# Decayed linear attention and a highway layer on one Trainium2 core: query layout, decay factors, store shapes and a new order of all engines

## The chip, the cores and the metric

The kernel runs on one core of a Trainium2 chip. The metric is the device time of one execution in microseconds. The engines of the core work side by side, each through its own queue in order: TensorE (PE; its weight loads are shown as PEld), VectorE (DVE), ScalarE (ACT), GpSimd (POOL) and SyncE (SP), which here only issues DMAs. Sixteen DMA engines move the data.

## The reference

Four batches, eight heads, 768 positions, 64 features a head, all in float32. `lam` holds one decay factor for each head.

```python
for b in range(nb):                       # strips of 64 positions
    intra = einsum('bhic,bhjc->bhij', qb, kb) * Dmask      # lam ** (i - j) for i >= j, else 0
    intra = einsum('bhij,bhjd->bhid', intra, vb)
    inter = einsum('bhid,bhde->bhie', qb * lam_pow, kv_state)
    out[:, :, sl] = intra + inter
    kv_state = lam_block * kv_state + einsum('bhsd,bhse->bhde', kb * rev_pow, vb)
...
x = out.transpose(0, 2, 1, 3).reshape(3072, 512)
H = maximum(x @ w_h, 0);  T = sigmoid(x @ w_t + b_t)
return T * H + (1 - T) * x
```

The decay between two positions is split in the kernels: queries are scaled by lam to the power of their position in the batch, values by its inverse, so that masks need only ones and zeros and the state needs no decay of its own.

## The kernel before, in words

The 3072 rows are worked on as twelve tiles n of 256 rows; three tiles make a batch. A tile has two halves b of 128 rows, and an operation on "p" 0 or 1 is on half of the heads, on 2 on all of them. What runs on which engine, and in which order, is written out by hand in the string `PLAN`: a loop at the end of the kernel reads its tokens one by one and calls the function that `DO` names, so each engine's queue holds its operations in the plan's order. `@` names the engine, `=` the PSUM banks (seven of them, 0 to 6). Buffers in SBUF are taken in turn, `BUFS` many of a kind; an operation that reuses one waits until the earlier use is over.

For one tile:

- `Lk`, `Lq`, `Lv` (line 173) load keys, queries and values, in two transfers of 256 KB each, as rows of 512 B (two positions of one head). All go through SP's queue, as do the weights (`W`, line 177) and the stores (`ST`, lines 337 and 356).
- `CK` casts the keys to bf16 (line 103 on DVE and POOL, 101 on ACT, which all copies share), `CQ` and `CV` scale queries and values by the decay factors (line 190).
- `TK`, `TQ` transpose keys and queries on TensorE (line 204) and `EK`, `EQ` copy the result from PSUM to `kT` and `qT`.
- `SS` is sixteen score matmuls (line 216) with sixteen matmuls of the running state `kv` between them (line 221), `KE` copies the state out to `ss`. For tile 0 scores and states stand apart as `S` and `U`. `M` masks the scores on DVE (line 255).
- `I` (line 271) and `A` (line 281) make the attention's output, transposed, in PSUM; `D` copies it to `xT`.
- `F.n.u.w` is a block of the highway layer for half of the features, eight matmuls (line 300; w is 0 for `w_h` and 1 for `w_t`). `H` makes max(h, 0) - x (line 305), `G` the sigmoid (line 314), `X` their product `th` (line 318). The last tile's halves are two groups, 11 and 12.
- `R` turns x + th back to rows by matmuls with the identity (line 347; 327 for the last tile), `E` copies them to `o`, `ST` stores them.

`WC` casts the weights, once. `Z.r` is r matmuls of a blank tile, which nothing reads (`spin`, line 366). `B` and `BC` make a column of the bias, `PT` loads the table for the sigmoid. Before the plan starts, lines 106 to 135 make the identity, the mask `tri` and the tables `pow_q` and `pow_v`: `lam` is loaded into all 128 partitions (line 107), its logarithm is multiplied with the positions (line 130), and two Exp follow (lines 133 and 135).

The PSUM tile of an attention output has its 128 columns in the order (parity of the position, pair), because a partition holds two neighbouring positions; `take` puts them in order:

```python
copy(eng, new(("xT", *g), ...)[:, :, r * C:(r + 1) * C].rearrange("p n (q j) -> p n j q", j=J),
     get("o", n, b).rearrange("p n (j q) -> p n j q", j=J))
```

Of the kernel before, what the change touches and what calls it, by code (L numbers as in the profile page):

```python
# [418 lines left out]
```

## Time and profile before

| | |
|---|---|
| median of 3 runs | 109.11 us (108.66 to 109.51) |
| profiled execution: span from its first to its last instruction | 109.3 us; the page gives no other time of it, and the span stands 0.2 us above the runs' median |
| granted TensorE clock, mean | 1.000 |
| HBM read and written | 20.98 MB and 6.29 MB, 249 GB/s over the span |
| `kf`, `vf`, `qf`: one load of 256 KB, issue to landing | 5.5, 5.4, 5.5 us |
| `w_f`: one load of 512 KB | 6.6 and 8.5 us |
| `out_dram<-o`: one store of 512 KB | 4.7 us |
| `m` on DVE, 48 times | 682 ns each |
| `qb` and `vs` on POOL, 128x1024 | 1904 ns each |
| `kT` and `qT` on ACT, 128x1024 | 1036 and 1023 ns |
| `xT` on ACT, 128x512 | 749 ns |

How to read the profile: an engine's digit is its busy share in one fortieth of the span. Matmuls are pipelined, so a busy TensorE may still have room. The chain of waits is followed back from the last instruction to what released each step. A group's line gives engine, operation, what it writes and reads, how often, busy time and mean, and the idle time before it with its releaser. A timeline line gives start, length, and the idle time before it in brackets.

### The profile page before, as it was taken

To read this page: it belongs to the slowest core of one execution; us is meant where nothing else is said; L and a number is where in the kernel's file an instruction comes from. 1 tells how busy PE (TensorE), PEld (TensorE's weight loads), DVE (VectorE), ACT (ScalarE), POOL (GpSimd) and SP (SyncE) were. 2 spreads that over 40 slices of the span, in tenths; PEclk is the share of its full clock that TensorE was granted. 3 is DMA by queue.
4 is the path that set the end of the run, shared out by engine and by line. 5 is a ranking of instruction groups with operands and counts; after the bars stand their busy time and mean duration, and the time that the engine had idled before them with its cause. 6 is when DMAs were issued, how large, how long until landed. Compare 5 with 4: busy or idle time off the path is not lost.

```text
span 109.3 us, 4968 instructions
## 1 busy us (share of the span) xinstructions
PE 99.4 (91%) x2188; PEld 80.6 (74%) x2190; DVE 82.7 (76%) x140; ACT 71.9 (66%) x129; POOL 55.7 (51%) x46
## 2 busy tenths in 40 slices
PE   4986989899999999999999999998999599999950
PEld 1343654688887878889899889896888478899940
DVE  1241595878998696999977989999858958958960
ACT  3304263787866489499579749975696758776940
POOL 6029420427979858959468296499691600000000
PEclk9999999999999999999999999999999999999999
DMA  0899999999999999989999999599999413207264
GB/s 5 233 304 290 291 366 386 312 290 287 290 266 304 287 250 262 302 228 289 296 300 293 305 341 270 181 346 326 321 333 323 170 69 125 73 6 296 94 233 151
DMA packets 42701, 27.59 MB, mean 252 GB/s; under 512 B 1588, under 2 KB 38712, under 8 KB 42680
## 3 DMA queue, kind: packets, MB, share of 16 engines
q1 hardware_dynamic: 42528, 27.27, 85.1%
q8 instruction: 17, 0.28, 1.2%
q14 instruction: 4, 0.03, 0.1%
q10 hardware_dynamic: 152, 0.01, 0.1%
HBM read 20.98 MB, written 6.29 MB: 249 GB/s over the span
## 4 chain that ended last, share of the span: by engine, by line
PE 61%; DMA 11%; DVE 6%; POOL 5%; ACT 5%; issue 4%; SPq 4%; POOLq 0%; DVEq 0%
PE bt L300 15%; PE bh L300 13%; DMA qf<-in_q_dram 11%; PE bs L216 7%; PE bo L281 5%; PE bx L347 5%; PE bspin L366 4%; PE bqtr L204 4%; DVE m L255 3%; SPq L173 3%; PE bktr L204 3%; POOL qb L190 3%; PE bo L271 3%; ACT qT L101 2%; POOL vs L190 2%
## 5 line engine op out<-in xcount | busy, mean ns | idle before, releaser
L300 PEld LDWEIGHTS <-w_b 128*128 128x128 bf16 x416 | 36.3, 98 | 6.4 <-issue 1.8
L255 DVE TENSOR_TENSOR m<-bs,tri 128x512 bf16<-128x512 f32 x48 | 31.1, 682 | 3.8 <-PE bs L216 3.4
L190 POOL TENSOR_TENSOR qb<-qf,pow_q 128x1024 bf16<-128x1024 f32 (+1 forms) x13 | 23.6, 1813 | 11.2 <-DMA qf<-in_q_dram 10.6
L314 ACT ACTIVATE bt<-bt,bt_col 128x256 f32<-128x256 f32 (+1 forms) x52 | 22.0, 432 | 6.9 <-PE bt L300 4.2
L300 PE MATMUL bt<-xT,w_b 128*128 128x256 bf16 (+1 forms) x208 | 24.5, 265 | 1.3 <-ACT qT L101 1.3
L300 PE MATMUL bh<-xT,w_b 128*128 128x256 bf16 (+1 forms) x208 | 25.0, 265 | 0.2 <-issue 0.2
L190 POOL TENSOR_TENSOR vs<-vf,pow_v 128x1024 bf16<-128x1024 f32 x10 | 19.0, 1904 | 5.0 <-DMA vf<-in_v_dram 4.6
L305 DVE SCALAR_TENSOR_TENSOR hm<-bh,xT 128x512 bf16<-128x512 f32 (+1 forms) x26 | 16.5, 643 | 4.0 <-PE bh L300 2.5
L318 DVE TENSOR_TENSOR th<-bt,hm 128x512 bf16<-128x512 f32 (+1 forms) x26 | 16.5, 643 | 2.1 <-ACT bt L314 2.0
L216 PE MATMUL bs<-qT,kT 64*64 64x128 bf16 x384 | 14.2, 218 | 0.6 <-issue 0.3
L101 ACT ACTIVATE xT<-bo 128x512 bf16<-128x512 f32 x16 | 11.5, 749 | 4.6 <-PE bo L281 4.6
L103 POOL CAST kb<-kf 128x1024 bf16<-128x1024 f32 (+1 forms) x10 | 10.0, 995 | 8.1 <-DMA kf<-in_k_dram 6.8
L101 ACT ACTIVATE ss<-kv 128x512 bf16<-128x512 f32 x15 | 8.9, 595 | 7.3 <-PE bs L216 6.1
L366 PE MATMUL bspin<-blank,id 128*128 128x512 bf16 x43 | 11.8, 416 | 1.6 <-POOL id masks.py:199 1.4
L216 PEld LDWEIGHTS <-kT 64*64 64x64 bf16 x384 | 11.0, 106 | 2.9 <-issue 1.4
L101 ACT ACTIVATE o<-bx 128x512 f32<-128x512 f32 x19 | 10.4, 596 | 1.4 <-PE bx L347 1.3
L101 ACT ACTIVATE qT<-bqtr 128x1024 bf16<-128x1024 bf16 (+1 forms) x10 | 9.8, 980 | 1.8 <-PE bqtr L204 1.8
L281 PE MATMUL bo<-m,vs 64*64 64x128 bf16 x384 | 9.4, 219 | 0.7 <-DVE m L255 0.4
L221 PE MATMUL kv<-vs,kb 64*64 64x64 bf16 x320 | 9.2, 196 | 0.2 <-POOL vs L190 0.2
L366 PEld LDWEIGHTS <-id 128*128 128x128 bf16 x45 | 4.3, 105 | 6.4 <-issue 1.7
L204 PE MATMUL bqtr<-id,qb 128*128 128x128 bf16 x96 | 7.5, 220 | 0.9 <-POOL qb L190 0.9
L281 PEld LDWEIGHTS <-vs 64*64 64x64 bf16 x384 | 6.6, 106 | 2.4 <-issue 1.5
(50 smaller groups left out, 109.1 us busy)
## 6 DMA issues: line engine op xcount, KB each, us to landing
kf<-in_k_dram SPq DMA_DIRECT2D x24, 256.0 KB, 5.5
vf<-in_v_dram SPq DMA_DIRECT2D x24, 256.0 KB, 5.4
qf<-in_q_dram SPq DMA_DIRECT2D x24, 256.0 KB, 5.5
out_dram<-o SPq DMA_DIRECT2D x11, 512.0 KB, 4.7
w_f<-in_moe_w_h_dram SPq DMA_DIRECT2D x2, 512.0 KB, 6.6
w_f<-in_moe_w_t_dram SPq DMA_DIRECT2D x2, 512.0 KB, 8.5
out_dram<-oh SPq DMA_DIRECT2D x2, 128.0 KB, 2.0
out_dram<-oq SPq DMA_DIRECT2D x1, 256.0 KB
```

What stands on the lines that cost most here:

```text
L101: A.activation(dst, src, AF.Copy)
L103: ENG[eng].tensor_copy(dst, src)
L190: ENG[eng].tensor_tensor(dst, in0=get(src, n)[:, heads(p)].rearrange("p h (j d) -> p h j d", j=J), in1=pw[:, n % NST, heads(p), :, None].t ...
L204: T.transpose(t[:, i, j, :], get(x + "b", n)[:, j, h:h + 2, :], id128)
L216: T.matmul(get("s", n, e, hp // 2)[half(b), hp % 2, j, :], lhsT=get("kT", n)[half(e), hp, j, half(b)], rhs=get("qT", n)[half(e), hp, :, ha ...
L255: V.tensor_tensor(new(("m", n, e, u), [128, 2, J, C]), in0=get("s", n, e, u), in1=tri[:, None].to_broadcast([128, 2, J, C]), op=ALU.mult)
L281: T.matmul(get("o", n, b)[half(e), hp, :], lhsT=get("vs", n)[half(b), 2 * hp + e, j, :], rhs=get("m", n, e, u)[half(b), hp % 2, j, :], sta ...
L300: T.matmul(t[:, r, :], lhsT=w_b[w][:, kc, (2 * u + r) * 128:(2 * u + r + 1) * 128], rhs=get("xT", *g)[:, kc, :], start=(kc == 0), stop=(kc ...
L305: V.scalar_tensor_tensor(new(("hm", g, u), [128, 2, z * C], tag=f"hm{z}"), in0=get("h", g, u), scalar=0.0, in1=get("xT", *g)[:, 2 * u:2 * ...
L314: A.activation(dst[:, r, :], src[:, r, :], AF.Sigmoid, bias=bt_col[:, 2 * u + r:2 * u + r + 1])
L318: ENG[eng].tensor_tensor(new(("th", g), [128, NP, z * C], tag=f"th{z}")[:, 2 * u:2 * u + 2, :], in0=get("tt", g, u), in1=get("hm", g, u), ...
L366: T.matmul(t, lhsT=id128, rhs=blank, start=True, stop=True)
```

## The change

- **Queries.** A partition now holds eight consecutive positions of one head, 2 KB in a row of `qf`; the four heads of one parity lie on neighbouring partitions. One load is 128 such rows instead of 512 rows of 512 B. `cast_q`, the transposes (`turned`) and `evac_q` follow: `qT` comes out in plain order of positions, so scores, masks (`tri`), `inter` and `take` work on plain columns.
- **Decay factors.** `lam` is loaded as a 4x2 tile. Two small float32 matmuls spread it over the partitions, once by head and once by the partition's number modulo 4; one Ln works on both. Queries get a table of their own, `pow_q8`.
- **Stores.** `ST.n@S` issues a tile's store as two DMAs, of 119 and 9 partitions; tiles 0, 1, 6, 7 and 8 have it.
- **Order.** `PLAN` is new from end to end: the order of the loads and stores on SP, which engine does which copy, the banks, and the place of every operation. There are 40 `spin` matmuls instead of 45, 34 of them ahead of the first transpose, where 12 were.

The new functions `load_wc`, `cast_wc`, `trans_rows`, `evac_k_rows`, `evac_q_rows` and `scores_state_intra` are not called by this plan; with this `GROUPS` the highway layer's groups are those of before. The core of the diff:

```diff
 PLAN = """
-Lk.0.0 Lv.0.1 Lv.0.0 Lq.0.0 Lk.0.1 Lq.0.1 Lv.1.1 CK.0.0@POOL Lq.1.0 Z.12=0 TK.0.0=0 Lq.1.1 CV.0.0@DVE Lk.1.0
-CQ.0.0@POOL EK.0.0@DVE Lv.1.0 CV.0.1@DVE CK.0.1@ACT Lk.1.1 Z.11=1 TQ.0.0=1 B=2 EQ.0.0@ACT CQ.0.1@POOL W.0.1 W.0.0
-Z.6=0 TQ.0.1=3 TK.0.1=4 EQ.0.1@DVE U.0.0 EK.0.1@ACT W.1.1 S.0.0=56 KE.0.0@DVE S.0.1=01 CQ.1.2@POOL W.1.0 M.0.0.1 Z.1=3
-U.0.1 I.0=34 M.0.1.1 KE.0.1@ACT Lk.2.1 M.0.0.0 A.0.1 M.0.1.0 TQ.1.2=0 Lq.2.1 CV.1.2@DVE CK.1.2@ACT EQ.1.2@ACT Lq.2.0
-Z.8=1 TK.1.2=1 A.0.0 EK.1.2@DVE Lk.2.0 D.0.0@DVE Z.3=5 SS.1.1=56 WC.0.0.1@ACT WC.0.0.0@POOL M.1.1.0 KE.1.0@ACT
-...
+Z.2=0 B=1 Z.2=2 Lk.0.1 Z.2=3 Lk.0.0 CK.0.0@ACT Lq.0.1 CQ.0.1@POOL CK.0.1@DVE Lq.0.0 CQ.0.0@DVE Z.3=4 Lv.0.1 Lv.0.0
+Lq.1.0 CV.0.1@POOL Lq.1.1 Lk.1.1 Lk.1.0 Z.2=5 Lv.1.0 Lv.1.1 Lq.2.0 Lq.2.1 BC@DVE Z.2=6 Z.5=0 Z.16=2 Lk.2.1 TK.0.0=3
+CQ.1.2@POOL TK.0.1=4 Lk.2.0 W.0.0 W.0.1 Z.6=5 TQ.0.2=6 Lv.2.0 EQ.0.1@ACT Lv.2.1 W.1.1 CV.0.0@DVE U.0.0 EQ.0.0@ACT
+CV.1.2@POOL EK.0.1@DVE S.0.1=02 W.1.0 Lq.3.1 EK.0.0@DVE CQ.2.2@POOL WC.0.1.1@POOL KE.0.0@DVE CV.2.2@POOL S.0.0=15
+U.0.1 KE.0.1@ACT WC.1.1.0@POOL Lq.3.0 Lk.3.1 M.0.0.1@DVE M.0.1.1@DVE WC.1.1.1@POOL Lk.3.0 Lv.3.0 WC.1.0.0@POOL I.0=46
+A.0.1 TQ.1.2=3 CK.1.2@ACT TK.1.2=0 EQ.1.2@ACT M.0.0.0@DVE M.0.1.0@DVE A.0.0 Lv.3.1 EK.1.2@ACT Lk.4.0 SS.1.1=21
+M.1.1.1@DVE D.0.1@ACT Lq.4.0 D.0.0@DVE KE.1.0@ACT CK.2.2@ACT SS.1.0=53 KE.1.1@ACT I.1=06 TK.2.2=1 WC.0.0.1@ACT
+M.1.1.0@DVE CQ.3.2@POOL M.1.0.0@DVE A.1.0 M.1.0.1@DVE WC.0.1.0@DVE A.1.1 D.1.0@DVE TQ.2.2=4 WC.0.0.0@ACT F.0.1.0=2
+H.0.1@DVE EK.2.2@DVE D.1.1@ACT F.1.0.0=5 EQ.2.2@ACT Lq.4.1 F.1.1.0=3 H.1.0@DVE SS.2.0=60 M.2.0.0@DVE SS.2.1=42
+M.2.1.0@DVE KE.2.0@ACT H.1.1@DVE F.0.0.0=1 I.2=56 M.2.1.1@DVE WC.1.0.1@ACT F.1.1.1=4 F.0.1.1=3 PT@ACT G.1.1@ACT
+F.1.0.1=2 A.2.0 G.0.1@ACT G.1.0@ACT M.2.0.1@DVE A.2.1 X.1.1@DVE X.0.1@DVE CK.3.2@POOL TQ.3.2=0 X.1.0@DVE F.0.0.1=4
+D.2.1@ACT G.0.0@ACT TK.3.2=3 EQ.3.2@ACT D.2.0@DVE F.2.1.0=6 R.1=25 E.1.1@ACT H.0.0@DVE CV.3.2@POOL X.0.0@DVE R.0=14
+...
+M.8.0.1@DVE H.6.1@DVE I.8=30 CQ.9.2@POOL TQ.9.2=4 F.7.1.0=2 Lv.9.0 CV.9.2@POOL ST.1@S F.7.0.0=5 H.7.1@DVE H.7.0@DVE
+...
+X.8.0@DVE M.11.1.0@DVE ST.5 F.8.1.1=0 F.9.1.1=2 M.11.0.1@DVE F.9.1.0=5 I.11=34 G.8.1@ACT X.8.1@DVE F.10.1.1=6
+F.10.1.0=0 ST.6@S H.9.1@DVE G.9.1@ACT G.9.0@ACT X.9.0@DVE A.11.0 X.9.1@DVE A.11.1 H.10.1@DVE D.11.0@ACT R.8=51 R.9=20
+F.10.0.0=3 E.8.0@DVE F.10.0.1=5 E.8.1@ACT D.11.1@ACT F.12.0.1=1 E.9.1@DVE H.10.0@DVE G.10.1@ACT X.10.1@DVE G.10.0@ACT
+G.12.0@ACT X.10.0@DVE F.12.0.0=4 H.12.0@DVE F.11.1.1=0 X.12.0@DVE F.11.0.1=3 F.11.0.0=6 ST.8@S H.11.0@DVE R.10=54
+E.9.0@ACT ST.9 G.11.0@ACT X.11.0@DVE R.11.1.0=2 G.11.1@ACT E.11.1.0@DVE F.11.1.0=1 E.10.1@ACT F.12.1.1=6 E.10.0@ACT
+ST.11.1.0 H.11.1@DVE X.11.1@DVE ST.10 F.12.1.0=3 R.11.0.2=2 G.12.1@ACT E.11.0.2@ACT H.12.1@DVE X.12.1@DVE R.11.1.1=4
+ST.11.0.2 E.11.1.1@ACT ST.11.1.1
 """
...
-    lam_bc = singles.tile([128, H], F32)
-    A.dma_start(out=lam_bc, in_=lam.partition_broadcast(128))
+    lam_r = singles.tile([NP, 2], F32)
+    A.dma_start(out=lam_r, in_=lam.rearrange("(h e) -> h e", e=2))
...
-    tri = singles.tile([128, J, J, C // J], F32)
+    tq_i = singles.tile([128, NST, Q], I32)
+    P.iota(tq_i, pattern=[[2 * C, NST], [1, Q]], base=0, channel_multiplier=0)
+    row_i = singles.tile([128, 1], I32)
+    P.iota(row_i, pattern=[[0, 1]], base=0, channel_multiplier=1)
+    tri = singles.tile([128, J, C], F32)
     P.memset(tri, 1.0)
     for b in range(2):
         P.affine_select(out=tri[half(b)], in_=tri[half(b)], compare_op=ALU.is_ge, fill=0.0, base=0,
-                        pattern=[[-1, J], [1, J], [J, C // J]], channel_multiplier=-J)
-    tri = tri.rearrange("p j i q -> p j (i q)")
+                        pattern=[[-1, J], [1, C]], channel_multiplier=-J)
...
+    V.tensor_scalar(row_i, in0=row_i, scalar1=128 - NP, scalar2=None, op0=ALU.bitwise_and)
+    row_f = singles.tile([128, 1], F32)
+    V.tensor_scalar(row_f, in0=row_i, scalar1=float(Q // NP), scalar2=None, op0=ALU.mult)
+    tq_f = singles.tile([128, NST, Q], F32)
+    V.tensor_scalar(tq_f, in0=tq_i, scalar1=row_f, scalar2=None, op0=ALU.add)
...
+    ones = singles.tile([NP, 128], F32)
+    V.memset(ones, 1.0)
+    pick = singles.tile([NP, 128 // NP, NP], F32)
+    V.tensor_copy(pick, id_f[:, None, :].to_broadcast([NP, 128 // NP, NP]))
+    lam_d = singles.tile([NP, NP, 2], F32)
+    V.tensor_tensor(lam_d, in0=id_f[:, :, None].to_broadcast([NP, NP, 2]), in1=lam_r[:, None, :].to_broadcast([NP, NP, 2]), op=ALU.mult)
+    lam_ps = ps.tile([128, H + 2], F32, tag="b6", name="lam_ps", bufs=1)
+    T.matmul(lam_ps[:, 0:H], lhsT=ones, rhs=lam_d.rearrange("k h e -> k (h e)"), start=True, stop=True, skip_group_check=True)
+    T.matmul(lam_ps[:, H:H + 2], lhsT=pick.rearrange("k p h -> k (p h)"), rhs=lam_r, start=False, stop=True, skip_group_check=True)
+    ln = singles.tile([128, H + 2], F32)
+    A.activation(ln, lam_ps, AF.Ln)
+    p_lq = singles.tile([128, NST, 2, Q], F32)
+    V.tensor_tensor(p_lq, in0=ln[:, None, H:H + 2, None].to_broadcast([128, NST, 2, Q]),
+                    in1=tq_f[:, :, None, :].to_broadcast([128, NST, 2, Q]), op=ALU.mult)
+    pow_q8 = singles.tile([128, NST, 2, Q], F32)
+    A.activation(pow_q8, p_lq, AF.Exp)
     p_ln = singles.tile([128, NST, H, J], F32)
-    V.tensor_tensor(p_ln, in0=ln_bc[:, None, :, None].to_broadcast([128, NST, H, J]),
+    V.tensor_tensor(p_ln, in0=ln[:, None, 0:H, None].to_broadcast([128, NST, H, J]),
                     in1=tk_f[:, :, None, :].to_broadcast([128, NST, H, J]), op=ALU.mult)
-    pow_q = singles.tile([128, NST, H, J], F32)
-    A.activation(pow_q, p_ln, AF.Exp)
...
+        if x == "q":
+            nc.sync.dma_start(out=new(("qf", n), [128, 2, Q * D], F32)[:, p],
+                              in_=q[b].rearrange("(h e) (c p j) d -> c e p h (j d)", e=2, p=C // NP, j=Q)[c, p])
+            return
...
-    def scale(n, p, eng, src, dst, pw):
+    def cast_q(n, p, eng):
+        es = slice(0, 2) if p == 2 else slice(p, p + 1)
+        z = es.stop - es.start
+        ENG[eng].tensor_tensor(new(("qb", n), [128, Q, 2, D])[:, :, es].rearrange("p j e d -> p e j d"),
+                               in0=get("qf", n)[:, es].rearrange("p e (j d) -> p e j d", j=Q),
+                               in1=pow_q8[:, n % NST, es, :, None].to_broadcast([128, z, Q, D]), op=ALU.mult)
+
+    def cast_v(n, p, eng):
         z = H if p == 2 else 4
-        ENG[eng].tensor_tensor(dst, in0=get(src, n)[:, heads(p)].rearrange("p h (j d) -> p h j d", j=J),
-                               in1=pw[:, n % NST, heads(p), :, None].to_broadcast([128, z, J, D]), op=ALU.mult)
-
-    def cast_q(n, p, eng):
-        scale(n, p, eng, "qf", new(("qb", n), [128, J, H, D])[:, :, heads(p)].rearrange("p j h d -> p h j d"), pow_q)
-
-    def cast_v(n, p, eng):
-        scale(n, p, eng, "vf", new(("vs", n), [128, H, J, D])[:, heads(p)], pow_v)
+        ENG[eng].tensor_tensor(new(("vs", n), [128, H, J, D])[:, heads(p)], in0=get("vf", n)[:, heads(p)].rearrange("p h (j d) -> p h j d", j=J),
+                               in1=pow_v[:, n % NST, heads(p), :, None].to_broadcast([128, z, J, D]), op=ALU.mult)
+
+    def turned(x, n, i):
+        if x == "k":
+            return get("kb", n)[:, i % J, 2 * (i // J):2 * (i // J) + 2, :]
+        return get("qb", n)[:, i]
 
     def trans(x, n, p, bk):
-        hs = heads(p)
-        t = bank((x + "tr", n, p), bk[0], [128, (hs.stop - hs.start) // 2, J, C], BF16)
-        for i, h in enumerate(range(hs.start, hs.stop, 2)):
-            for j in range(J):
-                T.transpose(t[:, i, j, :], get(x + "b", n)[:, j, h:h + 2, :], id128)
+        cs = range(8) if p == 2 else range(4 * p, 4 * p + 4)
+        t = bank((x + "tr", n, p), bk[0], [128, len(cs), C], BF16)
+        for i, c in enumerate(cs):
+            T.transpose(t[:, i], turned(x, n, c), id128)
...
     def evac_q(n, p, eng):
-        hs = heads(p)
-        copy(eng, new(("qT", n), [128, NP, J, C])[:, hs.start // 2:hs.stop // 2], get("qtr", n, p))
+        hs = slice(0, NP) if p == 2 else slice(2 * p, 2 * p + 2)
+        copy(eng, new(("qT", n), [128, NP, 2 * C])[:, hs].rearrange("e h (p j) -> e h p j", j=Q),
+             get("qtr", n, 2).rearrange("e j (p h) -> e h p j", h=NP)[:, hs])
...
     def score(n, e, hp, j, b):
         T.matmul(get("s", n, e, hp // 2)[half(b), hp % 2, j, :], lhsT=get("kT", n)[half(e), hp, j, half(b)],
-                 rhs=get("qT", n)[half(e), hp, :, half(b)], start=True, stop=True)
+                 rhs=get("qT", n)[half(e), hp, b * C:(b + 1) * C], start=True, stop=True)
...
-                             rhs=get("qT", n)[:, hp, :, half(b)],
+                             rhs=get("qT", n)[:, hp, b * C:(b + 1) * C],
...
     def take(n, b, eng):
-        g, r = groups(n, b)
-        z = 2 if len(g) == 1 else 1
-        copy(eng, new(("xT", *g), [128, NP, z * C], tag=f"xT{z}")[:, :, r * C:(r + 1) * C].rearrange("p n (q j) -> p n j q", j=J),
-             get("o", n, b).rearrange("p n (j q) -> p n j q", j=J))
+        g, z, r = groups(n, b)
+        copy(eng, new(("xT", g), [128, NP, z * C], tag=f"xT{z}")[:, :, r * C:(r + 1) * C], get("o", n, b))
...
-    def store_r(n):
+    def store_r(n, parts):
         i = 2 * n * C
-        nc.sync.dma_start(out=out[i:i + 2 * C].rearrange("(b p) f -> p b f", p=C), in_=get("o_sb", n).rearrange("p b j f -> p b (j f)"))
+        for p in parts:
+            nc.sync.dma_start(out=out[i:i + 2 * C].rearrange("(b p) f -> p b f", p=C)[p], in_=get("o_sb", n).rearrange("p b j f -> p b (j f)")[p])
...
+        "ST": lambda a, e, bk: store_r(*a, (slice(0, 119), slice(119, C)) if e else (slice(0, C),)) if len(a) == 1 else store(*a), "B": lambda a, e, bk: bias(bk), "Z": lambda a, e, bk: spin(*a, bk),
```

## The prediction

> **What bounds the kernel now.** I read the page's busy lines first, then the chain of waits, the windows, and the timelines of the first 20 us.
>
> ```profile
> PE 99.4 (91%) x2188; PEld 80.6 (74%) x2190; DVE 82.7 (76%) x140; ACT 71.9 (66%) x129; POOL 55.7 (51%) x46
> ...
> PE   4986989899999999999999999998999599999950
> ...
> DMA  0899999999999999989999999599999413207264
> ```
>
> TensorE is busy in almost every slice, but it is not doing the kernel's work in all of them: the first slices hold the matmuls of `spin` (L366, 43 in the records), which compute nothing. DMA is full until about 85 us.
>
> ```profile
> 9.68 0.40 PE bqtr L204 x4
> ...
> 22.09 1.75 PE bh L300 x16
> ...
> 63.33 6.45 DMA qf<-in_q_dram
> ...
> 69.93 1.44 POOL qb L190
> ...
> 72.82 1.87 POOL vs L190
> ```
>
> The columns of the chain are start, length, what. It runs through TensorE, except where it leaves it at 57 to 75 us: there a query load lands late, POOL scales late, and TensorE gets its operands late.
>
> ```profile
> core 0: us, PE busy (x) PEld busy (x) DVE busy (x) ACT busy (x) POOL busy (x), PEclk, DMA share, GB/s
> 15.00:20.00 5.00, 4.61 (x77) 2.73 (x77) 3.55 (x6) 2.66 (x4) 1.04 (x2) 1.00 1.06 379
> 25.00:30.00 5.00, 5.00 (x63) 4.42 (x62) 4.22 (x6) 3.99 (x9) 4.10 (x3) 1.00 1.09 288
> 40.00:65.00 25.00, 25.00 (x632) 22.11 (x631) 22.59 (x37) 19.42 (x34) 17.70 (x12) 1.00 1.03 289
> 70.00:75.00 5.00, 4.83 (x106) 4.22 (x94) 4.99 (x9) 3.92 (x6) 4.90 (x4) 1.00 1.07 339
> 75.00:80.00 5.00, 4.78 (x151) 4.18 (x139) 3.80 (x7) 3.12 (x8) 4.05 (x3) 1.00 1.05 334
> 80.00:85.00 5.00, 4.81 (x130) 4.05 (x128) 3.88 (x7) 3.81 (x6) 2.54 (x3) 1.00 0.94 313
> 85.00:90.00 5.00, 3.74 (x92) 3.05 (x90) 3.71 (x7) 3.20 (x6) 1.78 (x1) 1.00 0.33 120
> ```
>
> From 40 to 65 us TensorE has no pause at all; between 70 and 90 it pauses for 20 - 18.16 = 1.84 us. So the time is set by three things: when TensorE starts on real work without gaps, its fixed amount of work, and the pauses. The change leaves the matmuls as they are, so only the first and the last can move.
>
> **Queries in 2 KB rows.** Loads of 512 B rows alone ran at 288 GB/s (25 to 30 us); the stretch that is mostly weights, in 2 KB rows, at 379 (15 to 20 us). The queries are 24 x 256 KB = 6.29 MB: 21.8 us of full DMA before, 16.6 after, so 5.2 us less, 0.43 us a tile; the loads of tile 8 should land some 4 us earlier. Bounds: nothing, if the 379 came from the weights' own layout, to 5.2. Of this only what ends a TensorE pause counts. In 70 to 90 us POOL waited 2.4 us for queries and 2.4 us for values (chain: 69.93, 72.82), and TensorE behind it. The pauses there are 1.84 us by busy time; a pause also hides the drain of the last matmul (eight transposes take 0.61 us alone, 0.45 in the chain, so 0.16 each), and with some four pauses that makes 2.4 us. I take all of it off: -2.4, bounds 0 to -2.4.
>
> The Trainium skill (DMA: Bandwidth & Descriptors, Specifications) gives 512 B as the smallest transfer for line rate, which speaks against any gain. The trace does not agree: 288 against 379 GB/s. By that rule the term would be 0 and the sum 2.4 us higher.
>
> **Layouts that follow.** `take` becomes a plain copy: on ACT 749 ns before, the same shape unpermuted (`ss<-kv`) 595, so -0.15 each; on DVE 730 against 682. `evac_q` now reads PSUM with a stride and writes straight. No row shows a strided PSUM read; bounds 0 to the ratio that permuting cost `take`, 749/595 = 1.26, that is +0.26 us on a 1.02 us copy; I take the upper end, since it is the same engine and type. By counts and row durations DVE gets 3.0 us less in all (two more `kT`, four more `o`; one permuted `kb` of 1.63, two `ss`, three `qT` down to one, 1.9 us of `vs` moved to POOL), ACT between -1.0 and +2.2, POOL +1.6. DVE has 26 us and ACT 37 us of slack over the span, so this is worth nothing by itself, except near the DVE pauses of 30 to 40 us (PE busy 4.82 and 4.73 of 5): -0.7, bounds 0 to -0.9.
>
> **Decay factors.** A 4x2 load, two tiny matmuls, Ln, two products, two Exp take the place of a 128-row broadcast. The old load was issued at 0.80 and waited for until 4.42. The new one has 4 pieces; the shortest landing on the page (2.0 us, `oh`) gives 2.8, the old row 4.4. I take 2.9. Four steps of 0.2 us follow, so factors are there near 4.2, before the first query (8.05 before). Hidden by that load; without the cover it would cost the 1.3 us that ACT waited for `lam`. Eight more set-up instructions on DVE and POOL (0.1 to 0.25 us each, by `tk_f`) lie under the same wait. But the two matmuls stand first on TensorE, so the spins, which began at 1.43, now wait for `lam`: 2.9 + 0.2 (product) + 0.2 (matmuls) = 3.3 us.
>
> **The start of real work.** The plan puts 34 spins before the first transpose.
>
> ```profile
> 1.43 4.05 PE L366 MATMUL bspin<-blank,id 128*128 128x512 bf16 x12 [1.43 <-POOL id masks.py:199]
> ...
> 3.54 0.15 PEld L366 LDWEIGHTS <-id 128*128 128x128 bf16 x1 [0.28 <-issue]
> 3.96 1.02 PEld L366 LDWEIGHTS <-id 128*128 128x128 bf16 x5 [0.28 <-issue]
> ```
>
> Spins came 0.43 us apart until 4 us and 0.22 after, so the clock opened 2.6 us after the first. With the same delay: 6 slow ones to 5.9, then 28 x 0.217 = 6.1: real work starts at 12.0. From there I walked the queues with the row durations. Transposes, 6 spins (1.3) and query transposes end at 14.2; two `EQ` on ACT (0.76 each) 15.9; scores, and four masks on DVE (0.62 apart) to 18.2; ACT meanwhile has KE.0.1 to 17.3, CK.1.2 to 18.3, EQ.1.2 to 19.55, EK.1.2 to 20.5, all in one queue, so SS.1.1 stands until 20.5, and behind it everything on TensorE. KE.1.0 ends at 21.9, SS.1.0 at 22.4, DVE has masks and `D` to 23.85, then a mask and a weight cast to 24.85; TQ.2.2 ends and F.0.1.0 starts at 25.25. What this needs of loads (queries and keys of three tiles, values of two, `w_h`) is 5.2 MB, 18 us at 288 GB/s from 2.4 on, so DMA does not set it.
>
> TensorE has then done 6.8 us of real work (transposes of three tiles 6 x 0.45, scores and states 2.26, inter 0.67, intra 1.14). Before had done 5.3 at 22.09 (two tiles' transposes, one intra less), and with one and three quarters of its blocks of 0.87 us the same 6.8 at 23.6. The new order is behind by 25.25 - 23.6 = **+1.7 us**. From 25 us on I see no gap in either order until 34 us.
>
> **End.** From the last FFN matmul (104.1) to the end took 5 us, with one copy of 0.25 us on DVE inside the chain; that copy is now on ACT: -0.3, bounds 0 to -0.3.
>
> **Stores of 119 and 9.** Five stores become ten issues, 0.34 us more on SP each, while SP waits for evictions anyway (L356 waited 11.5 us for DVE): 0 in the sum; see the rival.
>
> **Sum.** Against the profiled execution's span: 109.3 + 1.7 - 2.4 - 0.7 - 0.3 = 107.6. The runs' median is 109.11, 0.2 below that span, so 107.4.
>
> **Rivals.** (1) *The pauses all go.* A tile's pitches in the chain are transposes 0.90, scores with states 1.14, inter 0.45, intra 0.57, four blocks 3.48, turns 0.57: 7.1 us. Twelve, less 1.7 for what the strips at a batch's ends lack and 0.6 for the last turns, make 83. With 6.8 done at 25.25 the other 76.2 end at 101.5, and with 4.7 behind it the span is 106.2, the time 106.0; with the clock open a microsecond earlier 105.0. Between them 105.4. For: 25 us without a pause at 40 to 65. Against: at the new loads' speed DVE and ACT queues still wait in order.
>
> (2) *The pauses stay.* If those at 70 to 90 come from the order of the queues and not from loads, 109.3 + 1.7 - 0.7 - 0.3 = 110.0, and half of them 108.8. For: the longest, 1.3 us, ended with `qT` on ACT. Against: POOL's 4.8 us of waiting for DMA just before.
>
> (3) *The clock opens late.* Each further slow spin costs 0.21 us; 8 more (T = 13.7) eat the gain: 109.1. For: the spins start 1.9 us later and the trace shows one opening only. Against: it took just 2.6 us.
> The Trainium skill (TensorE: Matmul & The Clock Gate, Part 1) says that the window of about 3.4 us runs freely, so the opening can take one to nearly two windows: 8 to 16 slow spins instead of 6, a sum of 107.8 to 109.5. The trace's 2.6 us is under that.
>
> (4) *Slower: a split store runs on few DMA engines.* No row shows a DMA of 119 partitions. If its partitions are shared out evenly, 119 = 7 x 17 lets 7 of 16 engines take 17 partitions each, 34 rows of 2 KB plus 2, where 128 partitions give each engine 16. At 379 GB/s a row takes 0.0865 us on an engine: 3.1 us instead of 1.4, +1.7 a store. Two places can put it on the path: ST.1 and ST.0, ahead of the last loads, and ST.8, ahead of the last stores. From two of five it decides: 107.4 + 3.5 = 110.9; with one it is even.
> The Trainium skill (DMA: Bandwidth & Descriptors, on why a DMA increments its semaphore by 16) has this rule: the largest number up to 16 that divides the partitions, so 7 and 9; no run here shows it yet.
>
> **Chances.** Forecast 0.40; (1) 0.15; (2) 0.15; (3) 0.10; (4) 0.20. Faster by over 1% (about what a measurement of this kernel tells from no change): the forecast, less a tenth that lands within 1%, and (1): 0.52. Within 1%: that rest, (3), and the milder halves of (2) and (4): 0.23. Slower: 0.25. Range 104.6 to 111.3: from a little under (1) to a little over (4). The forecast's own range is 106.2 to 108.6.
>
> **What would show it.** Right: `qf` landing well under 5.5 us; spins to about 12 us; first `bh` near 25; PE busy 5.00 in every window from 40 to 90; POOL waiting little for DMA. Wrong: first `bh` under 23 or over 27; pauses at 70 to 90 that no load ended; long landings of `out_dram`, or loads late behind ST.1.

## The result, and the profile after

The changed kernel is slower: 114.97 us, median of 4 runs (114.12 to 116.12), against 109.31 (108.66 to 110.01). The ratio is 1.049, with a 95% interval of 1.040 to 1.059. The forecast was 107.4. (Ratios here compare undisturbed executions only; medians are of all.)

An execution's time lies 1.7 to 2.2 us above its span in all runs of this case: the profiled execution of the changed kernel has a span of 112.6 us and a time of 114.3. So the profiled execution of before, with its span of 109.3, took about 111, some 2 us more than usual. The spans of 25 unprofiled runs of before are 106.5 to 109.6, mostly near 107.2.

The page of the changed kernel, busy shares and slices:

```profile
PE 99.7 (89%) x2189; PEld 81.4 (72%) x2189; DVE 82.6 (73%) x144; ACT 71.1 (63%) x131; POOL 57.1 (51%) x49
...
PE   0999989389999939999999999799999999999940
...
DMA  2999999999999999999998889676910016544693
```

TensorE starts later and is full from about 25 us on, but for two slices, at 40 and at 71 us, where it shows a 3 and a 7. DMA is no longer full after some 60 us. The windows show the same in figures (columns as for before):

```profile
core 0: us, PE busy (x) PEld busy (x) DVE busy (x) ACT busy (x) POOL busy (x), PEclk, DMA share, GB/s
...
40.00:45.00 5.00, 3.22 (x67) 2.79 (x66) 2.98 (x6) 2.43 (x5) 4.22 (x4) 1.00 1.14 318
40.00:65.00 25.00, 23.15 (x531) 20.03 (x530) 20.25 (x33) 17.22 (x31) 17.85 (x13) 1.00 1.04 299
70.00:75.00 5.00, 4.29 (x113) 3.82 (x110) 3.83 (x6) 3.68 (x8) 4.21 (x3) 1.00 0.70 220
75.00:80.00 5.00, 5.00 (x161) 4.45 (x160) 4.54 (x9) 3.32 (x6) 2.43 (x2) 1.00 0.77 223
80.00:85.00 5.00, 5.00 (x74) 4.36 (x68) 4.54 (x8) 4.03 (x9) 2.90 (x2) 1.00 0.35 129
85.00:90.00 5.00, 4.88 (x187) 4.33 (x188) 4.93 (x9) 3.96 (x7) 0.00 (x0) 1.00 0.03 7
```

Two of the forecasts can be read off. The loads do finish earlier: DMA is 0.70 busy at 70 to 75 us, where it was 1.07, and 0.35 at 80 to 85 instead of 0.94. And from 75 to 85 us TensorE has no pause any more. But there are new ones, 1.78 us at 40 to 45 and 0.71 at 70 to 75. The chain of waits says what the first was:

```profile
39.83 0.21 PE bs L283 x7
40.04 1.78 issue
41.82 0.19 PE kv L288
```

"issue" is time in which the engine waited for nothing that the profile shows. TensorE stopped after a score matmul of tile 3, the last but one, and went on, 1.78 us later, with a state matmul of the same `SS`, whose operands had been used by the matmuls before it.

The head, in the timeline of TensorE:

```profile
3.06 0.59 PE L148 MATMUL lam_ps<-lam_d,ones 4*128 4x8 f32 x2 [3.06 <-DVE lam_d L146]
...
4.00 1.03 PE L454 MATMUL bspin<-blank,id 128*128 128x512 bf16 x2
...
5.16 8.18 PE L454 MATMUL bspin<-blank,id 128*128 128x512 bf16 x32
13.17 0.61 PE L255 MATMUL bktr<-id,kb 128*128 128x128 bf16 x8
...
21.07 0.24 PE L283 MATMUL bs<-qT,kT 64*64 64x128 bf16 x1 [1.09 <-ACT kT L107]
...
22.43 0.19 PE L288 MATMUL kv<-vs,kb 64*64 64x64 bf16 x1 [0.73 <-ACT ss L107]
...
25.70 1.47 PE L387 MATMUL bh<-xT,w_b 128*128 128x256 bf16 x12
```

The spins run from 4.0 to 13 us, the first transpose comes at 13.17 (5.99 before), two waits for ACT follow at 21 and 22 us, and the first `bh` starts at 25.70.

### Where the 3.3 us between the two profiles are

I set both traces side by side at equal amounts of TensorE's real work (transposes and everything after them). The changed kernel is behind by 2.2 us at 26 to 34 us, by 1.8 at 38.7, by 3.3 at 42.8 (the pause above), by 4.0 at 60, by 5.0 at 73 (the second pause), by 2.6 to 2.8 after 92 (before had a pause of its own at 86), and by 3.3 at the end. So some 2 us of the 3.3 were there before the first of these pauses.

### What the pauses have in common

The page lists the DMA queues:

```profile
q1 hardware_dynamic: 33312, 27.27, 80.6%
q8 instruction: 17, 0.28, 1.1%
```

Queue q8 carried 17 packets of 16 KB in the whole span. The trace gives the start and length of each. TensorE ran some 4380 instructions (a weight load and a matmul each count as one), about 17 times 256. Counted along TensorE's stream, with the few semaphore instructions in it, every pause behind the head that no operand's writer ends, in all fourteen traces of this case, stands at a remainder of 190 to 193 modulo 256, and TensorE goes on 1.2 to 1.7 us after a packet's end. Those of the two profiles, but for two of under 0.5 us:

| kernel | pause begins, us | remainder | length, us | packet, us | from its end to going on |
|---|---|---|---|---|---|
| before | 75.32 | 191 | 0.44 | 73.39 to 74.38 | 1.38 |
| before | 81.00 | 191 | 0.41 | 78.44 to 79.86 | 1.54 |
| before | 86.13 | 191 | 1.47 | 85.29 to 86.17 | 1.43 |
| after | 39.82 | 193 | 2.00 | 39.03 to 40.22 | 1.60 |
| after | 71.15 | 193 | 0.93 | 69.69 to 70.74 | 1.33 |

(Lengths here are from the start of one instruction to that of the next; the profile's idle time is shorter by the run of the last matmul.) A packet starts up to 4.2 us after TensorE has passed the boundary before it (once 5.0), and takes 0.9 to 2.5 us. A pause is what these two and the 1.2 to 1.7 us behind the packet leave over the time that the 256 instructions took: for the one at 86.13, 3.89 + 0.88 + 1.43 - 4.72 = 1.48. So the faster 256 instructions pass, the more likely the next packet isn't there: the pauses of all traces came after 2.2 to 5.7 us, those of over 1.5 us after 2.2 to 3.9. In the changed kernel 256 instructions passed in 2.9 us just ahead of the pause at 39.82: 64 turns and two `SS` of 32 small matmuls each, with a single block between.

The longest pause of before, at 86.13 us, is put down to `qT` on ACT in the timeline of the matmuls. The weight load ahead of that matmul needs only `w_b`, cast long ago, and stood as well:

```profile
87.60 0.77 PEld L300 LDWEIGHTS <-w_b 128*128 128x128 bf16 x8 [1.43 <-issue]
```

### The profile page after: what moved, and what is told of

Its sections match the earlier page's. It is cut to its first block, busy times and chain, and to the rows that moved or that the text cites. A ratio compares the mean times of both kernels' runs of the same rounds, so it can differ in the third digit from the quotient of the medians.

```text
span 112.6 us, 4976 instructions
## 1 busy us (share of the span) xinstructions
PE 99.7 (89%) x2189; PEld 81.4 (72%) x2189; DVE 82.6 (73%) x144; ACT 71.1 (63%) x131; POOL 57.1 (51%) x49
## 4 chain that ended last, share of the span: by engine, by line
PE 80%; DVE 7%; ACT 5%; issue 3%; POOL 1%; DVEq 0%; POOLq 0%
PE bh L387 18%; PE bt L387 18%; PE bspin L454 9%; PE bs L283 8%; PE bo L362 6%; PE bqtr L255 5%; PE bx L434 5%; PE bktr L255 4%; PE bo L356 3%; DVE m L340 3%; PE kv L288 2%; ACT bt L401 2%; ACT qT L107 1%; DVE th L405 1%; ACT kT L107 1%
## 5 line engine op out<-in xcount | busy, mean ns | idle before, releaser
L237 POOL TENSOR_TENSOR qb<-qf,pow_q 128x1024 bf16<-128x1024 f32 (+1 forms) x12 | 22.0, 1830 | 11.9 <-DMA qf<-in_q_dram 10.0
L243 POOL TENSOR_TENSOR vs<-vf,pow_v 128x1024 bf16<-128x1024 f32 (+1 forms) x12 | 22.0, 1830 | 8.6 <-DMA vf<-in_v_dram 5.6
L107 ACT ACTIVATE qT<-bqtr 128x1024 bf16<-128x1024 bf16 (+1 forms) x12 | 11.3, 952 | 12.5 <-PE bqtr L255 12.3
L107 ACT ACTIVATE ss<-kv 128x512 bf16<-128x512 f32 x17 | 10.2, 597 | 10.5 <-PE bs L283 9.7
L107 ACT ACTIVATE xT<-bo 128x512 bf16<-128x512 f32 x17 | 9.9, 596 | 4.1 <-PE bo L362 3.5
L109 POOL CAST kb<-kf 128x1024 bf16<-128x1024 f32 x9 | 9.3, 1036 | 3.6 <-DMA kf<-in_k_dram 3.1
L454 PE MATMUL bspin<-blank,id 128*128 128x512 bf16 x40 | 10.7, 424 | 0.0
L107 ACT ACTIVATE o<-bx 128x512 f32<-128x512 f32 x15 | 8.5, 595 | 1.9 <-PE bx L434 1.8
L288 PEld LDWEIGHTS <-kb 64*64 64x64 bf16 x320 | 7.8, 107 | 0.3
L109 DVE COPY kT<-bktr 128x1024 bf16<-128x1024 bf16 (+1 forms) x8 | 4.9, 617 | 4.0 <-PE bktr L255 4.0
```

Of the source, the lines that this page charges most:

```text
L107: A.activation(dst, src, AF.Copy)
L237: ENG[eng].tensor_tensor(new(("qb", n), [128, Q, 2, D])[:, :, es].rearrange("p j e d -> p e j d"), in0=get("qf", n)[:, es].rearrange("p e ...
L243: ENG[eng].tensor_tensor(new(("vs", n), [128, H, J, D])[:, heads(p)], in0=get("vf", n)[:, heads(p)].rearrange("p h (j d) -> p h j d", j=J) ...
L288: T.matmul(kv[half(e), hp, half(e)], lhsT=get("kb", n)[half(b), j, 2 * hp + e, :], rhs=get("vs", n)[half(b), 2 * hp + e, j, :], start=firs ...
L454: T.matmul(t, lhsT=id128, rhs=blank, start=True, stop=True)
```

## The experiments

### Parts of the change by themselves

**The new code with the old order.**

```diff
-PLAN = (that of after)
+PLAN = (that of before, but both halves of tile 0's queries turned at once; - before, + this run:)
-... TQ.0.0=1 B=2 EQ.0.0@ACT CQ.0.1@POOL ... TQ.0.1=3 TK.0.1=4 EQ.0.1@DVE ...
+... B=2 CQ.0.1@POOL ... TQ.0.2=3 TK.0.1=4 EQ.0.0@ACT EQ.0.1@DVE ...
```

> The changed kernel's layouts, tables and lam chain with the order of before (plain stores; tile 0's queries are turned in one step, as the new layout needs). If the order is what costs (theory O): within 1% of before or faster by up to the 2.4 us of the prediction, 106.5 to 110 us. If the layouts, the 2 KB rows or the lam chain cost (theory L): 112 us or more. If the stores do (theory S): as O, since none is split here.

Measured: 115.34 us (112.40 to 117.06), ratio 1.035 (1.021 to 1.048); profiled span 110.7. At equal work it is 2.87 us behind before from 20 us on. The timeline of TensorE shows why:

```profile
3.06 0.59 PE L145 MATMUL lam_ps<-lam_d,ones 4*128 4x8 f32 x2 [3.06 <-DVE lam_d L143]
...
4.00 5.30 PE L451 MATMUL bspin<-blank,id 128*128 128x512 bf16 x12
```

All twelve spins run 0.43 us apart, half the speed of later ones; in before six did. They begin behind the matmuls of the factors, and then the clock takes until 8.7 us to open. So the new code costs time in the old order too.

**The old code with the new order**, stores whole:

```diff
-PLAN = (that of before)
+PLAN = (that of after, with ST.n for ST.n@S)
 def evac_q(n, p, eng):
...
+    hp = slice(hs.start // 2, hs.stop // 2)
-    copy(eng, ...[:, hs.start // 2:hs.stop // 2], get("qtr", n, p))
+    copy(eng, ...[:, hp], get("qtr", n, 2)[:, hp])
```

> The new order with the layouts, loads, tables and whole stores of before. O: 113 to 116 us, TensorE's first FFN block again near 25.5 us or later. L: near 109. S: near 109.5, since no store is split.

Measured: 117.87 us (116.15 to 118.47), ratio 1.070 (1.055 to 1.084); span 114.3, first `bh` at 25.99. The new order alone is at least as slow as the whole change. So neither part is free, and the two don't add up: 1.035 and 1.070 alone, 1.049 together.

**Whole stores.**

```diff
-... ST.1@S ... ST.0@S ... ST.7@S ... ST.6@S ... ST.8@S ...
+... ST.1 ... ST.0 ... ST.7 ... ST.6 ... ST.8 ...
```

> The changed kernel with whole stores in the same places. S: 112.5 us or less, so 2.5 us or more given back. O and L: within 1 us of the changed kernel's 115.

Measured: 118.04 us (115.70 to 119.24), span 115.6. But the trace is already more than 4 us behind before at 43 us, long ahead of the first of these stores: its pause at 39.80 is 2.85 us instead of 2.00. So this run tells nothing of the stores; the last experiment does.

**Without Z.16.**

```diff
-... Z.5=0 Z.16=2 Lk.2.1 ...
+... Z.5=0 Lk.2.1 ...
```

> The changed kernel without the 16 blank matmuls just ahead of the first transpose, so real work can begin near 9.7 us instead of 13.2. If the late start costs what it shows (theory O in its first part): 111.5 to 113 us, and the first FFN block some 3 us earlier. If something else holds TensorE by then (weights, casts in ACT's queue, or instruction packets): within 1 us of 115.

Measured: 113.86 us (111.19 to 115.42), between what the two sides expected; the profiled execution, with a span of 109.5, is the quickest of the four. The first transpose comes at 10.26 instead of 13.17, the first `bh` at 22.78 instead of 25.70: 2.9 us each. The pause at 39.8 is gone from its place; there is one of 1.20 at 38.36, in transposes 32 instructions further on in the program, and again at remainder 193.

### Tests of the two causes

After these the theory was: a late start, from spins behind the factors and too many of them, and instruction packets that come late.

**Four spins ahead of the factors.**

```diff
+    early = ps.tile([128, 512], F32, tag="b2", name="bearly", bufs=1)
+    for _ in range(4):
+        T.matmul(early, lhsT=id128, rhs=blank, start=True, stop=True)
     T.matmul(lam_ps[:, 0:H], lhsT=ones, ...)
...
-Z.2=0 B=1 Z.2=2 Lk.0.1
+B=1 Lk.0.1
```

> The changed kernel with four of its 34 blank matmuls put ahead of the two matmuls that spread the decay factors; their number stays. Theory (late start: TensorE idles until 3.06 us for the factors and the clock opens only some 3 to 4 us after its first matmuls): blank matmuls from 1.43 us, clock open near 4 to 5 instead of 7.3 us, first transpose at 10.5 to 11.3 instead of 13.17, first bh at 23 to 24 instead of 25.70, time 112 to 113 against 115.0. Rival (the head is held by loads and by POOL's products, not by the blank matmuls): the first transpose comes earlier, but first bh stays at 25 to 25.7 and the time at 114.5 to 115.5.

Measured: 117.56 us (115.02 to 119.73), span 115.5. Wrong in two ways. The clock didn't open earlier: the spins run 0.43 us apart until 7.5 us, 6.1 us after the first matmul, where before needed 2.7. So only the time of the moved spins is saved, 0.87 us (first transpose 12.31, first `bh` 24.83). And the pause in tile 3's scores grew to 2.94 us. Behind it the granted clock fell, in the windows (its column stands ahead of the DMA share):

```profile
40.00:42.00 2.00, 0.11 (x3) 0.11 (x2) 0.18 (x1) 0.00 (x0) 1.71 (x1) 0.89 1.00 319
42.00:44.00 2.00, 2.00 (x13) 1.40 (x13) 1.29 (x2) 0.60 (x1) 1.04 (x1) 0.50 1.19 312
44.00:46.00 2.00, 2.00 (x50) 1.80 (x48) 0.14 (x1) 1.65 (x3) 0.66 (x1) 0.76 0.93 290
46.00:48.00 2.00, 2.00 (x22) 1.64 (x19) 1.74 (x3) 1.48 (x4) 2.00 (x2) 1.00 0.90 266
```

From 42 to 46 us it was 0.50 and 0.76, so by an estimate 2 x 0.50 + 2 x 0.24 = 1.5 us more were lost.

**96 places further on in the stream.**

```diff
-Z.16=2
+Y.64=2        # 64 matmuls of 128 columns on the blank tile
```

> The changed kernel with the sixteen blank matmuls of Z.16 (32 instructions, 3.5 us) replaced by 64 blank matmuls of 128 columns (128 instructions, about 3.6 us): the same time in the head, but every later instruction of TensorE stands 96 places further on in its stream. Theory (TensorE's instructions come in packets of 256, and it stops where a packet is late): the pause of 2.00 us in the scores of tile 4 at 39.8 us and that of 0.93 us at 71.1 us do not come at those places of the program; pauses come 96 instructions earlier in it, at positions that again leave the remainder 191 to 193 modulo 256, and where 256 instructions pass in less than about 4 us (in the old trace that is near 81 us only); sum of such pauses 0.3 to 1.3 us instead of 3.2, span 110.5 to 111.8 instead of 112.6. Rival (those pauses belong to the data: keys, masks or states of that tile come late): they stay in the same matmuls of tiles 4 and 8, and the span stays at 112.5 to 113.

Measured: 113.69 us (111.97 to 114.40), ratio 1.030 (1.020 to 1.041) instead of 1.049, span 110.2. The pauses at both places, the last scores of tiles 3 and 8, are gone; of 3.20 us in sum there are 0.37 left, at 38.84 and remainder 192, 20 scores ahead of the old place (and not near 81 us, where one was expected to stay). In the windows:

```profile
40.00:45.00 5.00, 5.00 (x109) 4.27 (x108) 4.61 (x8) 3.84 (x8) 4.43 (x4) 1.00 1.11 317
40.00:65.00 25.00, 24.90 (x624) 21.47 (x623) 21.68 (x35) 18.71 (x35) 19.14 (x13) 1.00 1.02 295
...
70.00:75.00 5.00, 5.00 (x75) 4.56 (x64) 4.73 (x8) 4.37 (x9) 4.94 (x4) 1.00 0.90 261
```

25.00 - 24.90 = 0.10 us of pause where it was 1.85. This came although the first `bh` was 0.7 us later here, at 26.38. No operand of those scores was touched, so they had not been waiting for data.

**The new code with the old order and four early spins.**

```diff
-Z.12=0
+Z.8=0         # and the four early spins as above
```

> The changed kernel's code with the order of before (as in the run with the old plan), and four of its twelve blank matmuls ahead of the matmuls that spread the factors. Theory (the 2.9 us by which that run began late come from the blank matmuls behind the factors): first transpose at 6.5 to 7.2 us instead of 9.36, time 111.5 to 113 against its 115.3, so the layout and the factors alone cost 2 to 3 us at most. Rival (the products of the queries or their evacuation are what is late): real work starts earlier, but first bh and the time do not move, 114.5 to 116.

Measured: 113.12 us (112.42 to 114.87), ratio 1.032 (1.026 to 1.039). That is the ratio of its like, 1.035 (1.021 to 1.048), so a gain in time isn't shown, though the medians lie 2.2 us apart. The first transpose comes at 7.84 instead of 9.36, not at 7, and first `bh` at 23.60 instead of 24.79, 1.7 us behind before. Of that lead its trace loses 0.87 us at 26.70, where the blocks wait for a weight cast on DVE, and 2.7 us at packets, where the other lost 0.7. Here the layout itself shows: the query transposes need all heads of a tile, so they stand at 12.42 us, where before had the first half at 9.68.

**Three buffers for loads.**

```diff
-BUFS = dict(kf=5, qf=5, vf=5, ...
+BUFS = dict(kf=3, qf=3, vf=3, ...
```

> The changed kernel with three instead of five buffers each for loaded keys, queries and values, so that fewer loads are in flight at a time. Theory (a packet of instructions is late because it stands behind the loads in the DMA engines): between TensorE's passing a boundary and the start of the next packet there are 0.1 to 1 us instead of 1.8 to 3.9, the pauses at boundaries fall below 0.5 us in sum, and if no load comes late itself the time is 112 to 113. Rival (the delay of a packet has nothing to do with loads in flight): the delays stay at 2 us and more, the pauses at 2 to 3 us in sum, time 115. A third way is that loads become late for their casts: then pauses that end on DMA, and 116 to 120.

Measured: 118.16 us (115.59 to 120.61), ratio 1.061 (1.052 to 1.071). What was expected of fewer loads in flight didn't come: packets still start up to 4.2 us late, and the pauses sum to 4.9 us. But the run doesn't decide whether packets stand behind loads, as DMA was as full as ever up to 55 us (a share of 1.01 to 1.11). Counted over all fourteen traces, a packet starts 0.7 us after the boundary in the median where DMA is less than a tenth busy within half a microsecond of it (45 packets), and 2.3 us where it is full (136). So full DMA and late packets go together; what makes a packet late stays open.

### The same test on the kernel before

If an instruction's place in the stream costs time, shifting it must slow the kernel before, at places that can be told ahead.

```diff
-Z.11=1
+Z.3=1 Y.50=1  # 84 places; 50 matmuls of 64x64
+Z.7=1 Y.26=1  # 44 places
```

> The kernel before, with eight of the eleven blank matmuls ahead of the first queries (1.7 us, under a wait for POOL) replaced by fifty blank matmuls of 64x64: the same work and the same order, but every later instruction of TensorE stands 84 places further on. Theory (a packet of 256 instructions comes 4.1 to 4.9 us after TensorE passes the boundary before it): from the profile of before with its own pauses taken out, two stretches of 256 instructions now pass in 2.2 to 2.4 us, one ending near 55 us and one near 79 us of the old time; pauses of about 2.3 and 2.1 us there, at remainders 191 to 193 modulo 256, time 112 to 114 against 109.2. If a pause of over 2.5 us also lowers the granted clock for some us, as in the run with early blank matmuls, up to 116. Rival (the pauses are waits for data, and the place of an instruction in the stream is nothing): 109 to 109.7.

> As the run with 84 places, with 44: four blank matmuls of 512 columns replaced by 26 of 64x64. Theory: one or two pauses of 1.8 us in sum by the same reckoning, time 110.3 to 111.5, between before and the run with 84 places. Rival: 109 to 109.7, as the other.

Measured with 84: 114.07 us (112.22 to 116.07) against 109.16, ratio 1.033 (1.027 to 1.039); with 44: 112.73 (111.73 to 113.33), ratio 1.033 (1.029 to 1.038). The two pauses that were foretold, 2.3 us near 55 and 2.1 near 79, came: 2.07 at 55.89 and 1.63 at 79.05, both at remainder 190. TensorE's timeline and windows with 84 places:

```profile
55.78 0.33 PE L216 MATMUL bs<-qT,kT 64*64 64x128 bf16 x5
57.96 0.21 PE L216 MATMUL bs<-qT,kT 64*64 64x128 bf16 x1 [1.86 <-issue]
```

```profile
50.00:55.00 5.00, 5.00 (x158) 4.53 (x154) 4.92 (x9) 3.86 (x7) 2.96 (x3) 1.00 1.02 281
55.00:60.00 5.00, 3.14 (x93) 2.74 (x85) 2.18 (x4) 2.25 (x5) 4.13 (x4) 1.00 0.96 276
75.00:80.00 5.00, 4.32 (x156) 3.61 (x153) 5.00 (x10) 3.56 (x5) 3.83 (x3) 1.00 0.98 317
80.00:85.00 5.00, 4.31 (x50) 3.97 (x50) 2.42 (x4) 3.79 (x8) 2.18 (x2) 1.00 0.79 240
```

In before both stretches from 50 to 60 us were full:

```profile
50.00:55.00 5.00, 5.00 (x162) 4.47 (x155) 4.92 (x9) 3.69 (x6) 3.49 (x3) 1.00 1.03 287
55.00:60.00 5.00, 5.00 (x98) 4.58 (x95) 3.59 (x6) 4.45 (x8) 3.71 (x4) 1.00 1.14 295
```

With 44 places there are five pauses of 0.37 to 1.37 us, 3.7 in sum instead of the 1.8 foretold, and the time is over the 110.3 to 111.5 expected; here the size was off, not the kind. The rival, 109.0 to 109.7, is out.

### Both remedies in the changed kernel

```diff
+    (the four early spins as above)
-Z.16=2
+Y.64=2        # 64x64 here: 2.2 us instead of 3.5
```

> The changed kernel with both remedies: four blank matmuls ahead of the matmuls that spread the factors, and the sixteen of Z.16 replaced by 64 of 64x64, which take less time (estimated 2 to 2.5 us instead of 3.5). Theory (late start and late packets are the whole of the loss): first transpose near 11, first bh at 23 to 24 instead of 25.70, pauses at boundaries 0 to 1.6 us in sum instead of 3.2, span 107 to 109, time 109 to 111. Rival (the head is held by loads and evacuations once the blank matmuls are short): first bh at 24.8 as with early blank matmuls alone, time 111.5 to 112.5.

> As the run before it in this list (both remedies), with the five split stores issued whole. The theory on record of a split store running on 7 of 16 DMA engines: whole stores are faster by 0.5 to 3 us. Theory (the split does nothing for the path, and the 118.0 of the run with whole stores came from a longer pause at a packet): within 0.7 us of the run with split stores. Third (split stores leave gaps in which loads and packets pass): whole stores slower by 1 to 3 us, with packets that start later after about 58 us.

Measured: 113.00 us (110.76 to 116.68), ratio 1.021 (1.014 to 1.029), span 110.2; with whole stores 112.10 (110.82 to 113.54), ratio 1.023 (1.017 to 1.030), span 109.1. First `bh` at 24.18 and 24.19. So by the ratios the remedies take back a little over half of the loss (1.049 to 1.021 and 1.023), less than was expected: the pauses were still 2.9 and 1.5 us in sum, and less these the spans still lie 0.9 and 1.2 us above those of before. The intervals of the two runs overlap almost wholly: the shape of the stores does nothing to the time that can be measured here. None of these kernels beats the one before.

### One sum for all traces

| kernel | span | pauses at packets: sum (longest) | span less pauses | first `bh` |
|---|---|---|---|---|
| before | 109.3 | 2.8 (1.47) | 106.5 | 21.92 |
| before, 84 places | 110.7 | 4.4 (2.07) | 106.3 | 22.10 |
| before, 44 places | 109.9 | 3.7 (1.37) | 106.2 | 22.17 |
| without Z.16 | 109.5 | 2.6 (1.20) | 106.9 | 22.78 |
| both remedies | 110.2 | 2.9 (1.27) | 107.3 | 24.18 |
| both, whole stores | 109.1 | 1.5 (1.22) | 107.6 | 24.19 |
| after | 112.6 | 3.2 (2.00) | 109.4 | 25.70 |
| after, 96 places | 110.2 | 0.4 (0.37) | 109.8 | 26.38 |
| three buffers | 114.8 | 4.9 (1.82) | 109.9 | 26.17 |
| whole stores | 115.6 | 5.5 (2.85) | 110.1 | 25.58 |
| early spins | 115.5 | 5.4 (2.94) | 110.1 | 24.83 |
| new code, old order | 110.7 | 0.7 (0.69) | 110.0 | 24.79 |
| the same, early spins | 113.1 | 2.7 (1.24) | 110.4 | 23.60 |
| old code, new order | 114.3 | 2.6 (1.38) | 111.7 | 25.99 |

The four from "after" to "whole stores", with one order and nearly one head, scatter from 110.2 to 115.6; less the pauses they agree within 0.7. The first three do so within 0.3, at 106.4 or so. So the change costs 109.4 - 106.4 = 3.0 us beside the packets, most of it by its later start: without Z.16, with a start 2.9 us earlier, 2.5 of them are gone. The rest is packets: an execution of before has usually 107.2 - 106.4 = 0.8 us of pauses, by this reckoning, and the changed one 3.2 in its trace. That makes 3.0 + 2.4 = 5.4, beside a difference of 5.7 in the medians. The 0.8 is worked out; no trace of a usual execution of before is there to read it from.

The last four rows follow less closely. Early spins also lost the 1.5 us to the clock. The other three lie 3.6, 4.0 and 5.3 us above 106.4 with a first `bh` 2.9, 1.7 and 4.1 us later than before; in the last two of them the first blocks also waited 0.87 us for a weight cast on DVE. What is left of these sums isn't accounted for.

## Why the prediction was wrong, by its steps

- **The pauses at 70 to 90 us (-2.4): this step failed.** They were put down to late queries, because the chain left TensorE for a load at 57 to 75 us. The loads did come earlier, but three of the four pauses (0.44, 0.41, 1.47) had ended with packets of instructions; only the first, 0.41 at 74.32, had ended with POOL's `vs`. At the end the step is worth +1.1 in the traces (1.8 behind at 38.7, 2.9 at the last matmul): the new order has 3.2 us of packet pauses of its own, where before had 2.8, and the other 0.7 isn't accounted for. "PE busy 5.00 in every window from 40 to 90" fails at 40, 70 and 85 with 3.22, 4.29 and 4.88.
- **The base.** The sum was set against a profiled execution that was itself 2 us over the usual. Its span was read as if it were a time; the 1.7 to 2.2 us between the two were missing. Even the forecast span of 107.6 would have been a time of 109.3 to 109.8, no gain.
- **The start (+1.7): right in kind, 0.5 short.** Measured +2.2. The first `bh` came near the forecast (25.70 for 25.25) partly by luck, as the real work began 1.2 us later than forecast and slack in the head took up part of that: the matmuls of the factors took 0.94 us and not 0.2, eight slow spins came instead of six, and the first transpose was at 13.17 for 12.0.
- **30 to 40 us (-0.7):** measured -0.4 (2.2 behind, then 1.8).
- **The end (-0.3):** measured +0.4; ACT's copy in the tail takes 0.38 us for DVE's 0.42, but the wait behind the last matmul is 3.56 us for 3.20.
- **Queries in 2 KB rows (5.2 us of DMA): this held.** The queue's share times the span is 93.0 us before and 87.4 in the kernel with both remedies and whole stores:

```profile
q1 hardware_dynamic: 42528, 27.27, 85.1%
```

```profile
q1 hardware_dynamic: 33312, 27.27, 80.1%
```

The four traces with 512 B rows have 92 to 94 us, the four with 2 KB rows and whole stores 87 to 89, so rows of 512 B did cost. The median landing of a query load shows it less well: 5.5 before, 4.9 after, but 5.7 in the old order. The Trainium skill's 512 B (DMA: Bandwidth & Descriptors, Specifications) spoke against a gain in the loads, which these runs don't bear out; that the time gained nothing has another cause. POOL's wait for queries hardly fell: 10.0 us in all for 10.6.
- **Layouts.** `take` measured 596 ns for 595. The strided read of `evac_q` costs nothing on ACT: 1.02 us as before, where 1.28 was taken. On DVE, for which nothing was taken, the one such copy costs 1.22 us instead of 0.69 (before, then after):

```profile
L103 DVE COPY qT<-bqtr 128x1024 bf16<-128x1024 bf16 x2 | 1.4, 692 | 0.3 <-PE bqtr L204 0.3
```

```profile
L109 DVE COPY qT<-bqtr 128x1024 bf16<-128x1024 bf16 x1 | 1.2, 1215 | 0.0
```

What was not seen either is that a tile's query transposes now need all its heads.
- **Rivals.** (2), pauses that belong to the order, was nearest in kind; its price was too low as it, too, went by the pauses of before. (3), the clock, happened in part: some eight slow spins here, seven to ten in the five traces with this head. The free-running window that the Trainium skill states (TensorE: Matmul & The Clock Gate, Part 1) had led to an estimate of 8 to 16; the traces lie at its lower end and under it. (4), split stores, is out by the last two runs, though the sign named for it came: unsplit stores of 512 KB landed in 7.9 us, 4.7 before. The split does take DMA time, 90 to 91 us in the six traces that have it where whole stores took 87 to 89, but no time that the last two runs can tell. (1) fell with the -2.4.

The rule that bore on this most was not weighed: the Trainium skill says that crossing from one block of 256 instructions to the next is mostly hidden (Runtime: NRT & Kernel Launch, Instruction fetch mechanics). In these runs most of a trace's 17 crossings are hidden too, but one to five are not, and cost up to 2.9 us each.

## What to carry to other kernels

A pause that the profile calls "issue", in the middle of operands long at hand, is worth counting: if TensorE's instruction count there leaves the same remainder modulo 256 as at the next such pause, it most likely waits for instructions, and a faster copy won't shorten it. Many small matmuls in a row are where the long ones happen (here 256 instructions in 2.2 to 3.9 us), and a few blank matmuls more or fewer ahead can move the boundaries off them or onto them. Before a sum is made against a profiled execution, its span should be set beside the spans of the other runs, not beside their times.

## What the runs showed of the hardware

- A packet of 16 KB takes 0.9 to 2.5 us, and TensorE goes on 1.2 to 1.7 us after its end. Shifting the stream by 84 instructions cost the kernel before 3%.
- A pause of 2.94 us was followed by some 3 us at a granted clock of 0.5; pauses of 2.85 and 2.07 us were not. The idle window of about 3.4 us that the Trainium skill states (TensorE: Matmul & The Clock Gate, Part 1) is longer than all three, so the first does not agree with it.
- With the matmuls of the factors among the first spins the clock opened 6.1 to 7.4 us after the first matmul (four traces), without them 2.7 to 4.1 (three), and 6.6 where two spins were followed by 2.6 us of idle time (old code, new order). Where they came ahead of all spins it opened 4.2 to 5.7 us after the first of them (six). In the head the granted clock reads 1.00 all the while; only the spins' spacing, 0.43 against 0.22 us, shows the state.
